# Converting each weight block one step earlier, and one subtraction moved from VectorE to GpSimd

## The chip, the cores and the metric

The kernel runs on one core of a Trainium2 chip. The metric is device time in microseconds (us) of one execution; the median of the runs shown is compared. Engines go by the profile's names: PE (TensorE), PEld (its weight loads), ACT (ScalarE), DVE (VectorE), POOL (GpSimd), SP (SyncE, which issues the DMAs).

## The reference, cut to what matters

Attention within clusters is followed by two dense layers. Softplus sits between the two matrices of the first layer, a hard swish between those of the second. All data come as float64.

```python
mask = q_assign[:, :, :, None] == k_assign[:, :, None, :]
attn = softmax(where(mask, q @ k.T / sqrt(D), -1e9));  x = attn @ v     # 2 x 8 heads, 768 tokens, D = 64
x = (1536, 512)
x = softplus(x @ w_in) @ w_out                                          # 512 -> 2048 -> 512
h = x @ w_in2;  out = (h * clip(h + 3, 0, 6) / 6) @ w_out2              # 512 -> 2048 -> 512
```

## The kernel before

The attention runs first (about 0 to 268 us of the span), the first layer then to about 531 us, the second to the end.

**The layers.** The 1536 tokens are cut into 3 blocks of 512 and the 2048 hidden columns into 16 blocks of 128, f = 0 to 15. A step is one (layer, token block, f); there are 96, numbered n. In step n PE does `phase_a(n)`, 12 matmuls from x to the hidden block h, and then `phase_b(n - 2)`, 12 matmuls from the hidden block of two steps before to the output accumulators y. Every product of two float32 numbers is made of three passes: high times high, low times high, high times low. So each hidden block and each weight block is needed as a high part and a low part. In `phase_b` the third matmul is the first that reads the low part `glo` of the hidden block.

**The hidden block.** In the first layer ACT applies softplus twice (`g` and `ghi`, L830 and L831) and DVE subtracts to get `glo` (L844). In the second layer ACT, DVE, ACT and DVE work in turn (L833, L837, L841, L844).

**The weights** come as float64 pairs of 32-bit words (tiles `ri`, `ro` for block f of the first and the second matrix) and are converted on the chip. One conversion is, for each of the two matrices: `convert_abs` (ACT, L98), three `convert_bits` (DVE, L106, L108, L112), `convert_parts` (ACT, L122, the high part), `convert_rest` (L133, the low part by a subtraction). The results are `pi` and `po`. Blocks 0 to 2 of the first layer are converted during the attention, where L133 runs on POOL. Blocks 3 to 15 are converted in the first layer's first token block, block f in step f - 2, and those of the second layer in steps 38 to 59, about one in every 1.4 steps. In these 29 conversions both L133 run on DVE.

**The order.** `convert_at` says which block is converted in which step. The loop over n (L905 to L948) emits the work of a step in this order: `phase_a(n)`; L133 and the rest of the second matrix left over from the last step (`late`); bits, high part and low part of this step's first matrix (`ci`); bits of its second matrix (`co`); softplus; `convert_abs` for the next step; the last bits of `co`; and after all that `hid_lo(t)`, the DVE subtraction for `glo` of step n. `with tc.manual_schedule()` keeps that order on each engine, within the attention and within the layers. Between the two regions a scheduler merges the queues by what is ready. So the first steps of the layers run among the last instructions of the attention. Step 0 and step 1 have their `phase_a` done inside the attention. The softplus of every step is held behind the last transposed copy of the attention on ACT (`issue_after(last_flip[0].ins)`).

The fetches of blocks 7 to 15 (L90, on SP) stand before the loop, and their tiles lie where attention tiles lay. The pool of the converted words (`val1`) has four buffers, two for each conversion.

Of the kernel before, what the change touches and what calls it, by code (L numbers as in the profile page):

```python
# [22 lines left out]
def cluster_attention_then_two_mlps(  # L23
# [13 lines left out]
    nc = tc.nc  # L37
# [43 lines left out]
    def fetch_w(layer, f):  # L81

        w_in, w_out = (w_in1, w_out1) if layer == 0 else (w_in2, w_out2)
        pool = wpa if f < NFA else wpools["b" if f < NFB else "c"]
        for nm, src in (
            ("i", w_in.bitcast(U32)[:, 2 * f * P:2 * (f + 1) * P].rearrange("(c p) f -> p c f", p=P)),
            ("o", w_out.bitcast(U32)[f * P:(f + 1) * P, :].rearrange("p (c e) -> p c e", c=NC)),
        ):
            w = pool.tile([P, NC, P, 2], U32, tag=f"w{nm}{f}", name=f"r{nm}{f}")
            nc.sync.dma_start(w.rearrange("p c e w -> p c (e w)"), src)  # L90
            pieces[layer, f, nm] = [w]

    def convert_abs(layer, f, nm):


        w = pieces[layer, f, nm]
        val = wpools["val"].tile([P, NC, P], F32, tag="val", name="val")
        nc.scalar.activation(val, w[0].bitcast(F32)[:, :, :, 1], AF.Copy, scale=2.0**-112)  # L98
        w.append(val)
# [50 lines left out]
    def phase_a(n, c):  # L150
        layer, tb, f = steps[n]
        if c == 0:
            pl, tag = (ps_p, "prep") if n % 4 == 0 else (ps_h[0], "h")
            hs[n] = pl.tile([P, 512], F32, tag=tag, name="h")
        hi_w, lo_w = weights[layer, f, "i"]
        cols = slice(tb * TB, (tb + 1) * TB)
        for i, (w, x) in enumerate(((hi_w, xhi), (lo_w, xhi), (hi_w, xlo))):
            nc.tensor.matmul(  # L158
                hs[n][:, :TB], w[:, c, :], x[c][:, cols], start=(c == 0 and i == 0), stop=(c == NC - 1 and i == 2)
            )  # L160
# [666 lines left out]
    def hid_scalar(t):  # L827

        if t["layer"] == 0:
            nc.scalar.activation(t["g"], t["h"], AF.Softplus)  # L830
            nc.scalar.activation(t["ghi"], t["h"], AF.Softplus)  # L831
        else:
            nc.scalar.activation(t["u"], t["h"], AF.Relu, bias=half, scale=1.0 / 6.0)  # L833

    def hid_gate(t):
        if t["layer"] == 1:
            nc.vector.scalar_tensor_tensor(t["g"], t["u"], 1.0, t["h"], ALU.min, ALU.mult)  # L837

    def hid_hi(t):
        if t["layer"] == 1:  # L840
            nc.scalar.activation(t["ghi"], t["g"], AF.Copy)  # L841

    def hid_lo(t):
        nc.vector.tensor_tensor(t["glo"], t["g"], f32(t["ghi"]), ALU.subtract)  # L844

    def hidden(layer, h):
        t = {"h": h, "layer": layer}
        t["ghi"] = tmp.tile([P, TB], F32R, tag="ghi", name="ghi")
        t["glo"] = tmp.tile([P, TB], F32R, tag="glo", name="glo")
        t["g"] = tmp.tile([P, TB], F32, tag="g", name="g")  # L850
        if layer == 1:
            t["u"] = tmp.tile([P, TB], F32, tag="u", name="u", bufs=2)
        return t

    def phase_b(layer, f, g, ys):
        ghi, glo = g["ghi"], g["glo"]
        hi_w, lo_w = weights[layer, f, "o"]
        terms = ((hi_w, ghi), (lo_w, ghi), (hi_w, glo))
        for e, y in enumerate(ys):
            for n, (w, x) in enumerate(terms):  # L860
                fl = dict(start=(f == 0 and n == 0), stop=(f == NF - 1 and n == 2))
                if layer == 0:
                    nc.tensor.matmul(y[:, :TB], w[:, e, :], x, **fl)  # L863
                else:
                    nc.tensor.matmul(y, x[:, e * P:(e + 1) * P], w.rearrange("p c e -> p (c e)"), **fl)  # L865

    def finish_block(layer, tb, ys):
        cols = slice(tb * TB, (tb + 1) * TB)
        if layer == 0:
            for e in range(NC):  # L870
                y = ys[e][:, :TB]
                nc.scalar.activation(xhi[e][:, cols], y, AF.Copy)
                nc.vector.tensor_tensor(xlo[e][:, cols], y, f32(xhi[e][:, cols]), ALU.subtract)
        else:
            for t in range(TB // P):
                o = wpools["val"].tile([P, DM], F32, tag="val", name="o")
                if t % 2:
                    nc.vector.tensor_copy(o, ys[t])
                else:
                    nc.scalar.activation(o, ys[t], AF.Copy)  # L880
                c = tb * (TB // P) + t
                nc.sync.dma_start(out_v[c // NJ, c % NJ], o)
# [2 lines left out]

    convert_at = {}
    for f in range(NFA + 0, NF):
        convert_at.setdefault(f - 2, []).append((0, f))
    for f in range(NF):
        convert_at.setdefault((NB - 1) * NF + LAG + 4 + (7 * f) // 5, []).append((1, f))  # L890
    for f in range(NFB, NF):
# [1 line left out]
    with tc.manual_schedule():  # L893
        gs, ysd = {}, {}
        late = None
        pend = lambda n: {nm: (l, f, nm) for l, f in convert_at.get(n, ()) for nm in "io"}
        nxt = pend(0)
        for c in nxt.values():
            convert_abs(*c)

        def do(fn, x, *a, **kw):
            if x is not None:
                fn(*x, *a, **kw)

        for n in range(len(steps) + LAG):  # L905
            cur, nxt = nxt, pend(n + 1)
            ci, co = cur.get("i"), cur.get("o")
            ni, no = nxt.get("i"), nxt.get("o")
            t = None
            if n < len(steps):  # L910
                if n not in hs:
                    for c in range(NC):
                        phase_a(n, c)
                t = gs[steps[n]] = hidden(steps[n][0], hs.pop(n)[:, :TB])

            do(convert_parts, late, False)
            do(convert_bits, ci, 0)
            do(convert_bits, ci, 1)
            do(convert_rest, late, engine=nc.vector)
            do(convert_bits, ci, 2)  # L920
            do(convert_parts, ci, False)
            do(convert_bits, co, 0)
            do(convert_bits, co, 1)
            if t:

                with tc.issue_after(last_flip[0].ins):
                    hid_scalar(t)
            do(convert_rest, ci, engine=nc.vector)
            do(convert_abs, ni)
            if t:  # L930
                hid_gate(t)
            do(convert_bits, co, 2)
            if t:
                hid_hi(t)
                hid_lo(t)
            do(convert_abs, no)
            late = co
            if n >= LAG:
                l, tb, f = s = steps[n - LAG]
                if f == 0:  # L940
                    ysd[l, tb] = [
                        ps_y.tile([P, 512], F32, tag=f"y{e}", name=f"y{e}") for e in range(NC)
                    ]
                phase_b(l, f, gs.pop(s), ysd[l, tb])
                if l == 0 and tb == NB - 1:
                    fetch_w(1, f)
                if f == NF - 1:
                    finish_block(l, tb, ysd.pop((l, tb)))  # L948
# [35 lines left out]
```

## Time and profile before

| | |
|---|---|
| median of 3 runs | 793.37 us (793.04 to 794.87) |
| profiled execution | 795.4 us, its span 793.6 us |
| PE, DVE, ACT, POOL busy | 97%, 58%, 52%, 20% of the span |
| DVE in 300 to 350 us | 39.52 of 50 us |
| POOL after 272 us | nothing |

Durations of the trace are those of the one profiled execution. Instructions of one engine overlap a little in the records (a DVE subtraction of 512 columns lasts 0.68 us, and the next one starts 0.60 us after it), so that the distance between starts says what an instruction costs its engine. PE's matmuls are pipelined: one of 512 columns is recorded with 0.39 us, and they start 0.23 us apart.

### The profile page before, as it was taken

The page shows a single profiled execution, that of the slowest core. Times are in us where ns is not written, and L with a number is a line of the kernel's source. Part 1 is how long each engine was busy: PE and PEld are TensorE (multiplying, and loading weights), DVE is VectorE, ACT ScalarE, POOL GpSimd, SP SyncE. Part 2 cuts the span into 40 slices and gives each one's busy share as a digit, 9 for nine tenths or more (in the row PEclk, how much of TensorE's full clock was granted, in tenths as well). Part 3 has the DMA queues.
Part 4 walks back from the last instruction along what each step waited for, and adds up shares of the span by engine and source line. Part 5 has one row for each costly group of instructions (what it writes and reads, how often), then busy time and mean ns, then how long its engine had stood idle before and what let it go on. Part 6 is the DMA issues. An engine that isn't in the chain of part 4 may idle for free.

```text
span 793.6 us, 10533 instructions
## 1 busy us (share of the span) xinstructions
PE 772.8 (97%) x3829; PEld 645.7 (81%) x3829; DVE 462.1 (58%) x793; ACT 413.8 (52%) x827; POOL 155.0 (20%) x225
## 2 busy tenths in 40 slices
PE   6799999999999999999999999999999999999998
PEld 5688888888888778888888888888888888888886
DVE  4888888888898899921111257779852322232222
ACT  3689889889899766532121344555432222222221
POOL 3467568568423300000000000000000000000000
PEclk8899999999999999999999999999999999999999
DMA  6675484484375390000000265650000100010001
GB/s 156 192 202 136 127 193 110 128 198 109 83 173 190 127 370 1 1 0 1 1 0 1 82 208 178 196 185 1 1 1 0 54 1 0 1 54 0 1 1 53
DMA packets 37876, 69.75 MB, mean 88 GB/s; under 512 B 4384, under 2 KB 22464, under 8 KB 37824
## 3 DMA queue, kind: packets, MB, share of 16 engines
q1 hardware_dynamic: 37488, 68.91, 30.2%
q8 instruction: 30, 0.49, 0.2%
q10 hardware_dynamic: 336, 0.16, 0.1%
q14 instruction: 22, 0.18, 0.1%
HBM read 46.30 MB, written 3.19 MB: 62 GB/s over the span
## 4 chain that ended last, share of the span: by engine, by line
PE 85%; ACT 5%; DVE 4%; DMA 3%; issue 1%; POOL 1%; SPq 0%; ACTq 0%; DVEq 0%; POOLq 0%
PE h L158 32%; PE y L865 17%; PE y L863 16%; PE s L397 6%; PE t L427 6%; PE pv L442 6%; PE psm L297 2%; ACT pr L413 2%; DMA Q<-hiq 1%; ACT pth L431 1%; DMA K<-hik 1%; ACT mk L356 1%; DVE val L108 1%; ACT xs L455 0%; ACT xs L457 0%
## 5 line engine op out<-in xcount | busy, mean ns | idle before, releaser
L158 PE MATMUL h<-xhi,pi 128*128 128x512 f32 x768 | 238.8, 392 | 2.2 <-DVE pi L133 2.2
L158 PEld LDWEIGHTS h<-xhi,pi 128*128 128x128 f32 x768 | 143.7, 188 | 34.3 <-DVE pi L133 3.0
L844 DVE TENSOR_TENSOR glo<-g,ghi 128x512 fp32r<-128x512 f32 x96 | 66.3, 691 | 146.3 <-ACT ghi L831 117.5
L158 PE MATMUL h<-xlo,pi 128*128 128x512 f32 x384 | 150.0, 391 | 0.0
L863 PE MATMUL y<-ghi,po 128*128 128x512 f32 x384 | 118.9, 391 | 0.0
L865 PE MATMUL y<-po,ghi 128*128 128x512 f32 x384 | 118.8, 391 | 0.0
L432 DVE TENSOR_TENSOR ptl<-t,pth 128x384 fp32r<-128x384 f32 x192 | 97.9, 549 | 31.8 <-ACT pth L431 31.6
L837 DVE SCALAR_TENSOR_TENSOR g<-u,h 128x512 f32<-128x512 f32 x48 | 33.0, 687 | 127.2 <-ACT u L833 127.2
L833 ACT ACTIVATE u<-h,half 128x512 f32<-128x512 f32 x48 | 33.0, 686 | 128.3 <-PE h L158 128.1
L397 PE MATMUL s<-K,Q 128*128 128x256 f32 (+1 forms) x384 | 91.8, 361 | 4.5 <-ACT pr L413 3.2
L431 ACT ACTIVATE pth<-t 128x384 fp32r<-128x384 f32 x192 | 85.3, 487 | 17.7 <-PE t L427 17.3
L405 DVE TENSOR_REDUCE nm<-s 128x1 f32<-128x768 f32 x96 | 90.6, 944 | 3.1 <-PE s L397 3.0
L427 PE MATMUL t<-ident,pr 128*128 128x128 f32 x576 | 88.4, 282 | 2.1 <-DVE ptl L432 1.4
L413 ACT ACTIVATE pr<-s,nm 128x768 f32<-128x768 f32 x96 | 86.5, 901 | 3.6 <-DVE nm L405 3.3
L830 ACT ACTIVATE g<-h 128x512 f32<-128x512 f32 x48 | 28.5, 594 | 111.1 <-PE h L158 111.1
L863 PEld LDWEIGHTS y<-ghi,po 128*128 128x128 f32 x384 | 72.0, 188 | 15.7
L158 PEld LDWEIGHTS h<-xlo,pi 128*128 128x128 f32 x384 | 72.1, 188 | 15.6
L865 PEld LDWEIGHTS y<-po,ghi 128*128 128x128 f32 x384 | 72.1, 188 | 15.5
L427 PEld LDWEIGHTS t<-ident,pr 128*128 128x128 f32 x576 | 65.3, 142 | 19.7 <-DVE ptl L432 15.1
L397 PEld LDWEIGHTS s<-K,Q 128*128 128x128 f32 x384 | 67.0, 192 | 15.9 <-ACT pr L413 5.4
L865 PE MATMUL y<-po,glo 128*128 128x512 f32 x192 | 75.1, 391 | 0.0
L863 PE MATMUL y<-glo,po 128*128 128x512 f32 x192 | 75.0, 391 | 0.0
(125 smaller groups left out, 945.8 us busy)
## 6 DMA issues: line engine op xcount, KB each, us to landing
ri<-in_moe_w_in SPq DMA_DIRECT2D x32, 512.0 KB, 4.7
ro<-in_moe_w_out SPq DMA_DIRECT2D x32, 512.0 KB, 5.3
K<-hik SPq DMA_DIRECT2D x31, 192.0 KB, 4.7
Q<-hiq SPq DMA_DIRECT2D x15, 384.0 KB, 4.2
Q<-loq SPq DMA_DIRECT2D x16, 192.0 KB, 5.6
v<-in_v SPq DMA_DIRECT2D x8, 384.0 KB, 3.4
rsb<-row SPq DMA_DIRECT2D x16, 192.0 KB, 4.0
out<-o SPq DMA_DIRECT2D x12, 256.0 KB, 2.0
```

The lines of the kernel that those rows point to most:

```text
L158: nc.tensor.matmul(hs[n][:, :TB], w[:, c, :], x[c][:, cols], start=(c == 0 and i == 0), stop=(c == NC - 1 and i == 2))
L397: nc.tensor.matmul(ps[:, n0:n1], Q[i][:, u, j * P:(j + 1) * P], K[i][:, u, n0:n1], start=(u == 0), stop=(u == 1),)
L405: nc.vector.tensor_reduce(nm, st_s[t][:, :S], AX.X, ALU.max, negate=True)
L413: nc.scalar.activation(pr, st_s.pop(t)[:, :S], AF.Exp, bias=st_p[t], accum_out=sums_of[n][:, i, j:j + 1])
L427: nc.tensor.transpose(pt[:, c * P:(c + 1) * P], pr[:, kt * P:(kt + 1) * P], ident)
L431: last_flip[:] = [nc.scalar.activation(dh, src, AF.Copy)]
L432: nc.vector.tensor_tensor(dl, src, f32(dh), ALU.subtract)
L442: nc.tensor.matmul(st_v[h][:, :HALF], vs[:, kt, i, :], st_t[h][u][:, kt, :], start=(kt == 0 and u == 0), stop=(kt == NJ - 1 and u == 1),)
L833: nc.scalar.activation(t["u"], t["h"], AF.Relu, bias=half, scale=1.0 / 6.0)
L844: nc.vector.tensor_tensor(t["glo"], t["g"], f32(t["ghi"]), ALU.subtract)
L863: nc.tensor.matmul(y[:, :TB], w[:, e, :], x, **fl)
L865: nc.tensor.matmul(y, x[:, e * P:(e + 1) * P], w.rearrange("p c e -> p (c e)"), **fl)
```

## The change

`convert_at` puts blocks 3 to 15 of the first layer one step earlier: block f is converted in step f - 3, block 3 in step 0 instead of step 1. Its two `convert_abs` then stand ahead of the loop. The second layer's places stay as they were. In addition, the low part of the second matrix (`po`, for `late`) is made on POOL instead of DVE, in both layers.

```diff
     for f in range(NFA + 0, NF):
-        convert_at.setdefault(f - 2, []).append((0, f))
+        convert_at.setdefault(f - 3, []).append((0, f))
...
             do(convert_bits, ci, 1)
-            do(convert_rest, late, engine=nc.vector)
+            do(convert_rest, late, engine=nc.gpsimd)
             do(convert_bits, ci, 2)
```

## Rows read from the trace of the kernel before

**Rows 1.** The page, parts 1 and 4: busy time by engine; chain by engine.

```profile
PE 772.8 (97%) x3829; PEld 645.7 (81%) x3829; DVE 462.1 (58%) x793; ACT 413.8 (52%) x827; POOL 155.0 (20%) x225
...
PE 85%; ACT 5%; DVE 4%; DMA 3%; issue 1%; POOL 1%; SPq 0%; ACTq 0%; DVEq 0%; POOLq 0%
```

**Rows 2.** Waits of PE, 270 to 420 us: total, times, longest.

```profile
PE h L158 <- DVE pi L133: 2.2, 2, 1.1
```

**Rows 3.** Timeline of PE, 268 to 280 us: start, us, line, tiles, idle before.

```profile
268.69 0.62 PE L863 MATMUL y<-ghi,po 128*128 128x512 f32 x2
269.16 0.40 PE L863 MATMUL y<-glo,po 128*128 128x512 f32 x1
...
271.45 0.39 PE L158 MATMUL h<-xhi,pi 128*128 128x512 f32 x1
272.90 0.50 PE L158 MATMUL h<-xhi,pi 128*128 128x512 f32 x1 [1.06 <-DVE pi L133]
...
279.79 0.50 PE L158 MATMUL h<-xhi,pi 128*128 128x512 f32 x1 [1.10 <-DVE pi L133]
```

**Rows 4.** Timeline of DVE, 285 to 291 us, one step.

```profile
285.39 0.68 DVE L844 TENSOR_TENSOR glo<-g,ghi 128x512 fp32r<-128x512 f32 x1
...
287.06 0.68 DVE L133 TENSOR_TENSOR po<-val,po 128x512 fp32r<-128x512 f32 x1
287.66 0.69 DVE L112 SCALAR_TENSOR_TENSOR val<-ri,val 128x512 uint32<-128x512 uint32 x1
...
290.53 0.68 DVE L844 TENSOR_TENSOR glo<-g,ghi 128x512 fp32r<-128x512 f32 x1
```

**Rows 5.** Chain in order of time, two halves of a PE step.

```profile
290.93 2.80 PE h L158 x12
...
329.33 2.72 PE h L158 x12
```

**Rows 6.** Stretches: length, busy PE, PEld, DVE, ACT, POOL, clock, DMA.

```profile
255.00:260.00 5.00, 4.72 (x28) 3.59 (x27) 4.06 (x9) 4.57 (x11) 0.72 (x1) 1.00 0.00 0
260.00:265.00 5.00, 4.94 (x27) 3.88 (x25) 3.81 (x9) 4.32 (x8) 2.64 (x4) 1.00 0.00 0
...
500.00:600.00 100.00, 100.00 (x440) 82.21 (x439) 73.66 (x124) 49.62 (x84) 0.00 (x0) 1.00 0.22 69
...
265.60:337.00 71.40, 69.24 (x305) 56.34 (x304) 70.51 (x122) 44.61 (x84) 4.38 (x3) 1.00 0.38 139
```

**Rows 7.** Timeline of POOL, the same instruction alone and beside DVE.

```profile
249.99 1.28 POOL L133 TENSOR_TENSOR po<-val,po 128x512 fp32r<-128x512 f32 x1 [5.64 <-ACT po L122]
...
267.45 1.79 POOL L133 TENSOR_TENSOR po<-val,po 128x512 fp32r<-128x512 f32 x1 [4.81 <-ACT po L122]
269.20 2.63 POOL L506 TENSOR_TENSOR xlo<-xs,xhi 128x384 fp32r<-128x384 f32 x2
```

**Rows 8.** Timeline of DVE, 267 to 273 us, beside the POOL rows above.

```profile
267.39 0.69 DVE L112 SCALAR_TENSOR_TENSOR val<-ri,val 128x512 uint32<-128x512 uint32 x1
268.00 1.52 DVE L106 TENSOR_SCALAR val<-val 128x512 uint32<-128x512 uint32 x1
269.56 1.39 DVE L108 SCALAR_TENSOR_TENSOR val<-ro,val 128x512 uint32<-128x512 uint32 x1
270.88 1.37 DVE L460 TENSOR_TENSOR xs<-xs,xs 128x384 f32<-128x384 f32 x1
272.17 0.68 DVE L133 TENSOR_TENSOR pi<-val,pi 128x512 fp32r<-128x512 f32 x1
...
285.99 0.42 DVE L106 TENSOR_SCALAR val<-val 128x512 uint32<-128x512 uint32 x1
286.44 0.69 DVE L108 SCALAR_TENSOR_TENSOR val<-ri,val 128x512 uint32<-128x512 uint32 x1
```

**Rows 9.** Timeline of DVE, after the last bits of block 15.

```profile
336.76 0.68 DVE L844 TENSOR_TENSOR glo<-g,ghi 128x512 fp32r<-128x512 f32 x1
```

**Rows 10.** Timeline of PE, third matmul of step 14's second half.

```profile
337.78 0.39 PE L863 MATMUL y<-glo,po 128*128 128x512 f32 x1
```

## Prediction

> **What bounds the kernel now.** I read the busy times first, then the chain, then the waits of PE, then the timelines around the place where they point. PE is busy for 97% of the span and has 85% of the chain [rows 1]; so the change can only give back time in which PE stands still. From 270 to 420 us PE waited for one thing alone: twice for the low part of a first matrix `pi` (L133 on DVE), 2.2 us together [rows 2]. The timeline shows the places. Matmuls start 0.23 us apart, so the one after 271.45 was due at 271.68 and came at 272.90, 1.22 us late; the same happened to the one at 279.79, and since its recorded idle is 0.04 us longer I take 1.26 [rows 3]. These are blocks 3 and 4. Together 2.48 us, and that is the most that an earlier conversion can return. The layers after it have no wait of PE that the change touches.
>
> Why are the two late? From 265.6 to 337 us DVE is busy 70.51 of 71.40 us [rows 6]: it works off the 13 conversions without a pause. Its step is 290.53 - 285.39 = 5.14 us between two `glo` [rows 4]. PE's step is two halves of 2.80 us while the weights come in and of 2.72 us later, that is 5.60 and 5.44 us [rows 5]. So DVE is only 0.3 to 0.5 us a step faster than PE, and whatever slows it by more than that makes it the bound of this stretch.
>
> **Part 1, POOL takes one subtraction.** DVE loses one L133 per step, which costs it 287.66 - 287.06 = 0.60 us [rows 4]. POOL needs 1.28 us for the same instruction [rows 7] and is otherwise idle; `po` is needed only four steps later, so POOL's slowness itself costs nothing. What counts is what the POOL instruction does to DVE. The only place of this trace where POOL subtracts while DVE is working through conversions is 267.45 to 271.83 us. The POOL subtraction took 1.79 us instead of 1.28 [rows 7]. On DVE, L112 had started just before it and kept its 0.69 us; the next one, L106, took 1.52 us where 0.42 is normal, and ended 0.28 us after the POOL instruction did. Then L108 took 1.39 us against 0.69, and L460 1.37 us, 1.29 to the next start, each beside one of the two POOL instructions L506 [rows 7, 8]. So the two engines take turns: the one that is in goes through, the other stands. In distance between starts L106 cost 269.56 - 268.00 = 1.56 us against 286.44 - 285.99 = 0.45, so one POOL subtraction of 512 columns cost DVE 1.11 us [rows 8]; I take 1.10. The bounds: 0 if DVE came through as L112 did (less than nothing has no row and no reason), and the whole 1.28 us. I stay with 1.10, since it is the same instruction at the same size. Then a step of DVE is 5.14 - 0.60 + 1.10 = 5.64 us, 0.50 more than before and no longer below PE's 5.60 and 5.44.
>
> On this the Trainium skill has a rule, in "SBUF — State Buffer", section "SBUF: two separate sides": VectorE and GpSimd share a pair of ports, which one of them holds for its whole instruction while the other is fully blocked, and this includes VectorE instructions with two SBUF inputs. The trace agrees with the taking of turns; for the size the rule would have the full 1.28 us of [rows 7] rather than 1.10, and the sum below, 3.4 us, would be 12 x 0.18 = 2.2 us larger, the time 799.0.
>
> **Part 2, one step earlier.** On ACT, the two `convert_abs` of block 3 and its `convert_parts` now stand ahead of the softplus of step 0. On DVE a step's order is conversion first, `glo` last. So `pi` of block f now has one `glo` less in front of it. But `glo` of step n, which PE reads in step n + 2, now stands behind the conversion of block n + 3 instead of n + 2. The wait of PE moves from `pi` to `glo`, and the lead of a step is gone again: PE's `phase_b(n)` can't pass its third matmul before DVE has done conversions 3 to n + 3 and `glo` 0 to n. No DMA moves in its queue. Blocks 7 to 15 are fetched from before the loop, and the bits of the first of them begin four DVE steps (4 x 5.14 = 20 us) after those of block 3; I cost that at nothing.
>
> **The sum.** I take the last `glo` that stands behind a conversion: that of step 12, behind block 15. Before, DVE had done exactly this work (blocks 3 to 15 and `glo` 0 to 12) when the `glo` of step 13 started, at 336.76 [rows 9]; with the 0.08 us by which an instruction outlasts the distance of starts (0.68 - 0.60) it ended at 336.84. After the change 12 subtractions (`po` of blocks 3 to 14) leave it, 12 x 0.60 = 7.2 us, and 12 turns of POOL come in, 12 x 1.10 = 13.2 us: 342.84. Against this stands what DVE can do before 265 us, since block 3 is now free to start among the last steps of the attention. DVE idles 5 - 4.06 = 0.94 us from 255 to 260 and 5 - 3.81 = 1.19 us from 260 to 265 [rows 6]; 2.1 us is the upper bound, 0 the lower (block 3 not pulled ahead). The three bits of block 3's first matrix cost 0.45 (285.99 to 286.44), 0.62 (286.44 to 287.06) and 0.60, 1.67 us [rows 4, 8], and fit there; I take 1.7. So `glo` of step 12 ends at 341.14, and 0.05 us later (as 272.17 + 0.68 to 272.90 [rows 3, 8]) PE can go on: 341.19. Before, PE ran that matmul at 337.78 [rows 10]. The change makes it later by 3.4 us. Behind it no conversion is left in the block and DVE soon catches up, so PE runs without a wait from there, and the 3.4 us stay to the end.
>
> In these 3.4 us the old 2.48 us are included: without any wait PE would be at 335.30, so the new waits for `glo` should add up to 5.9 us, spread from 269 to 336 us, the larger share early. I expect about 2 us at the first `phase_b` steps already, since PE wanted `glo` of step 0 at 269.16 [rows 3], and DVE has the attention's tail and three POOL instructions to get past then.
>
> In the second layer's conversions (16 more POOL subtractions) DVE loses the same 0.50 us each, 8 us in all, but it is busy there for 73.66 of 100 us [rows 6], and 8 us spread over some 120 us are covered by that idle time. If the cover were gone, it would be these 8 us.
>
> The sum is made in the profiled execution (795.4 us, span 793.6), which would become 798.8. The median of the runs, 793.37, is 2.0 us under it; I move it by the same 3.4 us: 796.8.
>
> **Rivals.** For all of them the shift is 3.4 + 12 x (price of a POOL turn - 1.10) - (work pulled ahead - 1.7), and at least -2.5. What a measurement of this kernel can tell from no change is about 0.3%, 2.4 us.
>
> *POOL shares rather than blocks, and the time falls.* If a POOL subtraction cost DVE 0.60 us or less, as much as it takes off, DVE would keep its 5.14 us step, both waits would vanish, and the time would be 793.4 - 2.5 = 790.9. It is faster at all below a price of 0.82. For it: L112 of [rows 8] lost nothing. Against it: the two behind it lost 1.1 and 0.7 us.
>
> *The turns are partly covered.* POOL may often get its turn where DVE waits anyway; at 0.90 us a turn the shift is +1.0, that is 794.4, no change. For it: the attention's tail is irregular. Against it: DVE has 0.9 us idle in 71 us [rows 6].
>
> *Block 3 isn't pulled ahead.* If the merge of the two regions leaves its conversion where it was (because the buffer of its words is free only when the attention's last tiles are), part 1 works and part 2 does nothing: 3.4 + 1.7 = 5.1, 798.5. For it: ACT is busy for 4.57 and 4.32 of 5 us there [rows 6], and softplus waits in the same queue.
>
> **How the numbers follow.** Slower by 2.4 us or more (a turn of 1.02 to 1.28 us, 796 to 799): 0.50. Block 3 not pulled ahead: 0.08. Partly covered, within 2.4 us: 0.32. Full gain: 0.10, of which some lies just within 0.3%. So slower 0.58, same 0.34, faster 0.08. The likeliest case has 795.8 to 799.0 for itself. The range, 791.9 to 799.5, takes in the covered cases and most of the bounds of the two unknown costs (1.28 us a turn gives 799.0).
>
> **What would show it.** Right: DVE instructions of 1.4 to 1.6 us beside each L133 on POOL from 268 to 337 us; a DVE step near 5.64 us; PE waiting at L863 for `glo` (L844) instead of at L158 for `pi`. Wrong: PE without a wait after 268 us, or DVE instructions that keep their 0.42 and 0.69 us beside POOL, or waits of PE for `pi` that stay.

## The result and the profile after

The changed kernel takes 798.74 us (median of 4 runs, 797.8 to 799.6) against 793.96 us for the kernel before on the same chip (median of 4 runs, 793.04 to 794.87). The ratio is 1.0058 with a 95% interval of 1.0044 to 1.0072, that is 4.6 us (3.5 to 5.7) more. It is slower, as forecast: 796.8 us had been forecast (3.4 us more), in a range of 791.9 to 799.5.

The page after, parts 1 and 4, which answer to [rows 1].

```profile
PE 776.3 (97%) x3829; PEld 645.9 (81%) x3829; DVE 465.7 (58%) x764; ACT 413.8 (52%) x827; POOL 197.9 (25%) x254
...
PE 86%; ACT 6%; DMA 3%; DVE 3%; issue 1%; POOL 1%; SPq 0%; ACTq 0%; DVEq 0%; POOLq 0%
```

DVE has 29 instructions less and yet 3.6 us more of busy time: what is left on it became longer. POOL has 42.9 us more.

The waits of PE and of its weight loads from 255 to 420 us in the changed kernel (columns as in [rows 2]).

```profile
PE y L863 <- ACT ghi L831: 1.8, 1, 1.8
PE y L863 <- DVE glo L844: 1.1, 1, 1.1
...
PEld y L863 <- DVE glo L844: 4.9, 13, 1.5
PEld y L863 <- ACT ghi L831: 2.3, 1, 2.3
```

The waits for `pi` of [rows 2] are gone. In their place the second half of a step (L863) waits. PE itself stood twice, once for softplus (`ghi`) and once for `glo`; its weight loads waited 13 times for `glo`, once for each of the first 13 steps' hidden blocks. One DVE step of the changed kernel, and POOL beside it:

```profile
283.89 0.69 DVE L844 TENSOR_TENSOR glo<-g,ghi 128x512 fp32r<-128x512 f32 x1
284.49 0.42 DVE L106 TENSOR_SCALAR val<-val 128x512 uint32<-128x512 uint32 x1
284.94 0.69 DVE L108 SCALAR_TENSOR_TENSOR val<-ri,val 128x512 uint32<-128x512 uint32 x1
285.67 1.66 DVE L112 SCALAR_TENSOR_TENSOR val<-ri,val 128x512 uint32<-128x512 uint32 x1
287.25 0.41 DVE L106 TENSOR_SCALAR val<-val 128x512 uint32<-128x512 uint32 x1
...
289.51 0.68 DVE L844 TENSOR_TENSOR glo<-g,ghi 128x512 fp32r<-128x512 f32 x1
```

```profile
285.13 1.65 POOL L133 TENSOR_TENSOR po<-val,po 128x512 fp32r<-128x512 f32 x1 [4.71 <-DMA ri<-in_moe_w_in]
```

L112 takes 1.66 us where it had 0.69 in [rows 4]; it ends 0.55 us after the POOL subtraction has ended. The step is 289.51 - 283.89 = 5.62 us. Taken over the eleven steps from the `glo` of step 1 to that of step 12 it is (340.22 - 278.25) / 11 = 5.63 us; forecast 5.64, before 5.14.

```profile
278.25 0.68 DVE L844 TENSOR_TENSOR glo<-g,ghi 128x512 fp32r<-128x512 f32 x1
...
340.22 0.69 DVE L844 TENSOR_TENSOR glo<-g,ghi 128x512 fp32r<-128x512 f32 x1
```

So a turn of POOL costs DVE 5.63 - 5.14 + 0.60 = 1.09 us. The forecast had read 1.10 off L106; here L108 is the instruction held in the first two turns and L112 in the other ten, at the same price.

The start of the layers on PE, which answers to [rows 3], and on ACT:

```profile
269.80 0.73 PE L863 MATMUL y<-ghi,po 128*128 128x512 f32 x2 [1.85 <-ACT ghi L831]
271.61 0.50 PE L863 MATMUL y<-glo,po 128*128 128x512 f32 x1 [1.08 <-DVE glo L844]
```

```profile
260.87 0.66 ACT L98 ACTIVATE val<-ri 128x512 f32<-128x512 f32 x1
...
265.71 0.63 ACT L122 ACTIVATE pi<-val 128x512 fp32r<-128x512 f32 x1 [0.66 <-ACT po L122]
...
267.37 1.28 ACT L830 ACT_TABLE_LOAD   x1
268.66 0.60 ACT L830 ACTIVATE g<-h 128x512 f32<-128x512 f32 x1
```

The softplus of step 0 stands behind `convert_parts` of block 3 (L122). That one starts when the last bits from DVE are done (265.62; the profile names an ACT instruction, which had ended before):

```profile
264.93 0.69 DVE L112 SCALAR_TENSOR_TENSOR val<-ri,val 128x512 uint32<-128x512 uint32 x1
```

Two instructions of the attention and the loading of softplus's table follow, and softplus starts at 268.66. In the kernel before, the same ACTIVATE was at 263.35:

```profile
263.35 0.60 ACT L830 ACTIVATE g<-h 128x512 f32<-128x512 f32 x1
```

And TensorE's granted clock, in stretches of 1 us of the changed kernel (columns as in [rows 6]):

```profile
271.00:272.00 1.00, 0.39 (x2) 0.35 (x3) 0.97 (x3) 0.63 (x1) 0.25 (x1) 1.00 1.03 395
273.00:274.00 1.00, 1.00 (x4) 0.71 (x4) 0.96 (x2) 0.00 (x0) 0.04 (x1) 0.50 1.06 371
276.00:277.00 1.00, 1.00 (x6) 0.78 (x6) 1.00 (x3) 1.00 (x3) 0.00 (x0) 1.00 1.08 399
```

PE had stood 2.93 of the 3.66 us from 267.95 to 271.61. From about 272 us the clock was at 0.50, the lower of its two levels (1.2 GHz), for some 3.4 us, and matmuls started 0.43 us apart instead of 0.23.

**A common zero.** Between two executions the first 260 us differ by up to 2.4 us, between kernels with the same attention too. So the traces below are laid on each other at the last transposes of the attention on PE (before and after):

```profile
260.95 0.49 PE L427 MATMUL t<-ident,pr 128*128 128x128 f32 x3
```

```profile
259.89 0.49 PE L427 MATMUL t<-ident,pr 128*128 128x128 f32 x3
```

The table gives, for each kernel, how much later than in the kernel before PE starts the second half (`phase_b`) of hidden block m, counted from that point; m = 18 lies behind the last conversion of the first layer. Of the runs it gives the ratio and its interval, and the shift in us that the ratio means. The columns by m come from one profiled execution of each kernel. Those of softplus first and of the memset were 1.4 and 1.2 us faster than the median of their runs, so that there the two kinds of column differ most.

| kernel | m = 0 | m = 4 | m = 12 | m = 18 | runs: ratio (95%), us |
|---|---|---|---|---|---|
| the change, both parts | +2.17 | +2.97 | +4.23 | +4.40 | 1.0058 (1.0044 to 1.0072), +4.6 |
| earlier only | +2.16 | +3.49 | +3.49 | +3.49 | 1.0041 (1.0029 to 1.0054), +3.3 |
| POOL only | +0.02 | +0.69 | +1.96 | +2.15 | 1.0032 (1.0020 to 1.0045), +2.5 |
| softplus first in step 0 | -0.01 | +5.90 | +5.90 | +5.90 | 1.0090 (1.0074 to 1.0107), +7.1 |
| POOL in the second layer only | +0.02 | +0.01 | +0.01 | +0.01 | 1.0011 (1.0003 to 1.0020), +0.9 |
| earlier only, PE kept at work | +2.24 | +2.48 | +2.48 | +2.48 | 1.0028 (1.0018 to 1.0039), +2.2 |
| both, PE kept at work | +2.23 | +3.03 | +4.25 | +4.44 | 1.0054 (1.0040 to 1.0068), +4.3 |
| both subtractions on POOL | +2.17 | +5.22 | +10.46 | +11.14 | 1.0148 (1.0135 to 1.0162), +11.8 |
| second matrix one step behind | -0.03 | -2.43 | -2.43 | -2.43 | 0.9974 (0.9964 to 0.9985), -2.1 |
| memset in the place of POOL's subtraction | +2.17 | +1.85 | +1.85 | +1.85 | 1.0035 (1.0023 to 1.0047), +2.8 |

### The profile page after: what moved, and what is told of

It is laid out like the page before. It is cut to its first block, busy times and chain, and to the rows that moved or that the text cites. A ratio compares the mean times of both kernels' runs of the same rounds, so it can differ in the third digit from the quotient of the medians.

```text
span 796.9 us, 10584 instructions
## 1 busy us (share of the span) xinstructions
PE 776.3 (97%) x3829; PEld 645.9 (81%) x3829; DVE 465.7 (58%) x764; ACT 413.8 (52%) x827; POOL 197.9 (25%) x254
## 4 chain that ended last, share of the span: by engine, by line
PE 86%; ACT 6%; DMA 3%; DVE 3%; issue 1%; POOL 1%; SPq 0%; ACTq 0%; DVEq 0%; POOLq 0%
PE h L158 32%; PE y L863 17%; PE y L865 17%; PE s L397 6%; PE pv L442 6%; PE t L427 6%; PE psm L297 2%; ACT pr L413 2%; DMA Q<-hiq 1%; ACT pth L431 1%; ACT xs L455 1%; DMA K<-hik 1%; ACT mk L356 1%; DMA K<-mk 0%; ACT val L98 0%
## 5 line engine op out<-in xcount | busy, mean ns | idle before, releaser
L844 DVE TENSOR_TENSOR glo<-g,ghi 128x512 fp32r<-128x512 f32 x96 | 66.5, 693 | 145.4 <-ACT ghi L831 116.6
L863 PE MATMUL y<-ghi,po 128*128 128x512 f32 x384 | 120.3, 395 | 1.8 <-ACT ghi L831 1.8
L133 POOL TENSOR_TENSOR po<-val,po 128x512 fp32r<-128x512 f32 x32 | 46.9, 1465 | 289.0 <-ACT po L122 143.2
L863 PEld LDWEIGHTS y<-ghi,po 128*128 128x128 f32 x384 | 72.6, 189 | 17.7 <-ACT ghi L831 2.3
L863 PE MATMUL y<-glo,po 128*128 128x512 f32 x192 | 76.9, 401 | 1.1 <-DVE glo L844 1.1
```

What stands on the lines that cost most here:

```text
L133: engine.tensor_tensor(lo, val, f32(hi), ALU.subtract)
```

## The experiments

**Earlier only.** The changed kernel with the subtraction back on DVE.

```diff
-            do(convert_rest, late, engine=nc.gpsimd)
+            do(convert_rest, late, engine=nc.vector)
```

> Only the earlier conversion (block f in step f - 3), all subtractions on DVE. Theory: the loss is the turns of POOL on a DVE that has no idle time, so without them DVE keeps its step of 5.14 us and stays ahead of PE; what remains is the wait at the first second half (1.85 + 1.08 us in the changed kernel) in place of the old two waits for pi (2.48 us): about +0.4 us on the kernel before, 794.3. Rival: the earlier place itself costs, by the softplus that waits behind block 3 in ACT's queue and the glo behind one more conversion: then +4 or more stays, about 798.

Measured +3.3 us, 797.02: the theory fell. The rival was right that the earlier place itself costs, though not quite its +4. The waits of PE (1.85 for `ghi`, 1.04 for `glo`) are those of the changed kernel, and the clock stood at 0.50 here too, for some 6.8 us:

```profile
273.00:274.00 1.00, 1.00 (x4) 0.71 (x4) 1.00 (x3) 0.96 (x2) 0.00 (x0) 0.50 1.08 432
```

DVE's step is 5.14 us and from m = 4 on nothing is added, so DVE without POOL's turns keeps up.

**POOL only.** The kernel before with the other half of the change.

```diff
-            do(convert_rest, late, engine=nc.vector)
+            do(convert_rest, late, engine=nc.gpsimd)
```

> Only the subtraction of the second matrix on POOL, block f still in step f - 2. Theory: DVE's step grows by 0.49 us (1.09 for a turn of POOL, less 0.60), over 12 steps 5.9 us; the pi of block 15 had 4.0 us in hand before, so PE comes 1.9 us later: 795.8, with waits of PE for pi (L133 on DVE) through the whole block and none for glo. Rival: the start-up makes the loss, not POOL: then 793.9, no change.

Measured +2.5 us, in the trace +2.15. As the theory has it, PE's weight loads waited 13 times for `pi`, in all 6.5 us against 3.0 us twice in the kernel before, and never for `glo`:

```profile
PEld h L158 <- DVE pi L133: 6.5, 13, 2.0
```

**Softplus first in step 0.** The changed kernel; the softplus and the `glo` of step 0 stand ahead of block 3's conversion, and its two `convert_abs` behind them.

```diff
...
+            if n == 0:
+                with tc.issue_after(last_flip[0].ins):
+                    hid_scalar(t)
+                hid_lo(t)
+                for c in cur.values():
+                    convert_abs(*c)
             do(convert_parts, late, False)
...
-            if t:
+            if t and n:
...
-                hid_lo(t)
+                if n:
+                    hid_lo(t)
```

> The changed kernel, but in step 0 softplus and the glo of the hidden block are queued ahead of block 3's conversion. Theory: DVE's work up to the glo of step 12 is the same, so the end stays where it is, at 798 to 800, though the wait at the first second half (2.9 us) is gone; PE waits for glo later and more often instead. Rival: the start-up wait of 2.9 us adds to the rest, and without it the time is 795.8.

800.83 us, a ratio of 1.0090 against the change's 1.0058: the rival is out, and the theory too. The end did not stay where DVE's work up to step 12 sets it. The whole +5.90 is there by m = 4 and POOL's turns add nothing to it, and the weight loads waited for `glo` once instead of 13 times. The wait at m = 0 is gone, but larger ones stand a step later, since the softplus of step 1 still is behind block 4's `convert_parts`. The clock stood at 0.50 here too, from about 277 us on for some 6.8 us.

```profile
271.01 0.50 PE L158 MATMUL h<-xhi,pi 128*128 128x512 f32 x1 [1.04 <-DVE pi L133]
276.21 0.73 PE L863 MATMUL y<-ghi,po 128*128 128x512 f32 x2 [2.37 <-ACT ghi L831]
279.12 0.80 PE L863 MATMUL y<-glo,po 128*128 128x512 f32 x1 [2.18 <-DVE glo L844]
```

**POOL in the second layer only.**

```diff
-            do(convert_rest, late, engine=nc.vector)
+            do(convert_rest, late, engine=nc.gpsimd if late and late[0] else nc.vector)
```

> The kernel before, with the subtraction on POOL in the second layer's 16 conversions only. Theory: DVE instructions grow to 1.6 us beside POOL there too, but DVE idles a quarter of that stretch, so no change, 793.9 within 0.5 us. Rival: a late glo reaches PE in the steps with conversions in a row, up to 8 us (16 x 0.49): 795 to 802.

The trace shows what the theory says: the first matrix's L112 grew to 1.22 us in the mean, and PE had no wait in the second layer. It agrees with the kernel before to 0.01 us at m = 18, and its span of 791.6 us, with 2.0 us less ahead of the common zero, ends at the same point as the 793.6 of before. The runs say +0.9 us with an interval of 0.2 to 1.6; where that came from the trace doesn't show, and it stays open.

```profile
L112 DVE SCALAR_TENSOR_TENSOR val<-ri,val 128x512 uint32<-128x512 uint32 x15 | 18.4, 1224 | 0.5
```

**Earlier only, PE kept at work.** Nine matmuls without use stand ahead of the first second half.

```diff
+                if n == LAG:
+                    for _ in range(9):
+                        nc.tensor.matmul(
+                            ysd[l, tb][3][:, :TB], weights[0, 0, "i"][0][:, 0, :], xhi[0][:, :TB], start=True, stop=True
+                        )
                 phase_b(l, f, gs.pop(s), ysd[l, tb])
```

> Only the earlier conversion, as in the run that made +3.4 us, with nine idle matmuls (9 x 0.23 = 2.05 us, into an accumulator bank that is started afresh afterwards) put ahead of the first second half, where PE waits 1.85 us for softplus. Theory: of the 3.4 us some 2.5 us are TensorE's clock, which after that wait stood at 0.50 for 6 us (matmuls 0.43 us apart instead of 0.23); with PE kept at work the clock stays at 1.00 and the time falls to about +0.9: 794.5. Rival: the clock is no matter, the wait itself and DVE make the 3.4: 797.

795.99 us, between the two. The clock stayed at 1.00, and 1.0 us came back in the trace (3.49 to 2.48), not 2.5, because a wait appeared that the slow clock had hidden: `glo` of step 1, behind the conversion of block 4.

```profile
270.97 0.50 PE L863 MATMUL y<-glo,po 128*128 128x512 f32 x1 [1.10 <-DVE glo L844]
277.98 0.50 PE L863 MATMUL y<-glo,po 128*128 128x512 f32 x1 [1.20 <-DVE glo L844]
```

**Both parts, PE kept at work.** The same nine matmuls in the changed kernel.

> The changed kernel (both parts) with the same nine matmuls. Theory: the start-up loss and the turns of POOL don't add, the larger sets the end; DVE's work up to the glo of step 12 is what it was, so though the clock stays at 1.00 the time stays near that of the change, 797.5 to 799, with more waits for glo in the steps after 276 us. Rival: the losses add, and without the clock's share it is 2 us faster: 796.5.

798.06 us, as the theory has it. The clock stayed at 1.00, and still m = 18 comes at +4.44 against +4.40. So 1.0 us less of start-up loss, as in the part alone, changes nothing at the end here: the losses don't add, and DVE's work sets the end.

```profile
273.00:274.00 1.00, 1.00 (x6) 0.81 (x5) 1.00 (x2) 0.25 (x1) 0.00 (x0) 1.00 1.10 425
```

**Both subtractions on POOL**, in the first layer.

```diff
-            do(convert_rest, ci, engine=nc.vector)
+            do(convert_rest, ci, engine=nc.vector if ci and ci[0] else nc.gpsimd)
```

> The changed kernel with the subtraction of the first matrix on POOL as well, in the first layer. Theory: a second turn of POOL per step, DVE's step is 4.54 - 0.60 + 2 x 1.09 = 6.1 us; over 12 to 13 steps 5.9 to 6.4 us more, all of it seen by PE: 804 to 806. Rival: POOL's turns are covered or shared: at most 800.

805.73 us, inside the theory's range. A DVE step is 297.91 - 291.77 = 6.14 us, and two of its instructions are long:

```profile
291.77 0.68 DVE L844 TENSOR_TENSOR glo<-g,ghi 128x512 fp32r<-128x512 f32 x1
292.38 0.41 DVE L106 TENSOR_SCALAR val<-val 128x512 uint32<-128x512 uint32 x1
292.82 1.67 DVE L108 SCALAR_TENSOR_TENSOR val<-ri,val 128x512 uint32<-128x512 uint32 x1
...
296.31 1.68 DVE L112 SCALAR_TENSOR_TENSOR val<-ro,val 128x512 uint32<-128x512 uint32 x1
297.91 0.68 DVE L844 TENSOR_TENSOR glo<-g,ghi 128x512 fp32r<-128x512 f32 x1
```

**Second matrix one step behind.** A version of the kernel before that takes work out of the way of the first `pi`, instead of moving a whole block.

```diff
     for f in range(NFA + 0, NF):
-        convert_at.setdefault(f - 2, []).append((0, f))
+        convert_at.setdefault(f - 2, []).append((0, f, "i"))
+        convert_at.setdefault(f - 1, []).append((0, f, "o"))
     for f in range(NF):
-        convert_at.setdefault((NB - 1) * NF + LAG + 4 + (7 * f) // 5, []).append((1, f))
+        for nm in "io":
+            convert_at.setdefault((NB - 1) * NF + LAG + 4 + (7 * f) // 5, []).append((1, f, nm))
...
-        pend = lambda n: {nm: (l, f, nm) for l, f in convert_at.get(n, ()) for nm in "io"}
+        pend = lambda n: {c[2]: c for c in convert_at.get(n, ())}
```

> A version that should beat both: all on DVE, the first matrix of block f in step f - 2 as before, its second matrix a step later, in f - 1 (it is needed in step f + 2). DVE has the same work but 3 to 4 instructions less ahead of the pi of blocks 3 and 4. Theory: both waits for pi (2.48 us) go and nothing comes in: 791.2. Rival: DVE has no idle time, so the wait only moves to a glo or a po: 793.7.

791.76 us, 0.9974 of the kernel before: the best version here. Of PE's waits for `pi` only two short ones of the weight loads are left, and the whole 2.4 us came back by m = 4.

```profile
PEld h L158 <- DVE pi L133: 0.6, 2, 0.4
```

**A memset on POOL.**

```diff
+        if nm == "o" and (layer == 1 or f >= NFA):
+            engine.memset(f32(lo), 0.0)
+            return
         engine.tensor_tensor(lo, val, f32(hi), ALU.subtract)
```

> The changed kernel with a memset of the same tile on POOL in the place of the subtraction (this leaves out the low part of the second matrices), so that POOL writes the 512 columns and reads nothing. Theory: only the start-up loss is left, which was 3.4 us with DVE alone, since DVE's step falls to 4.54 us and a little: 797. Of DVE's instructions those with two inputs (L108, L112, L133, 0.69 us) keep their time beside it. Rival: any instruction of POOL stops DVE for as long as it lasts: then single DVE instructions grow by the length of the memset, the time being 797 to 798.5.

797.34 us, which lies in the theory and in the rival alike; the single instructions decide. The memset lasts 0.53 us, and DVE's subtraction for `glo` beside it keeps its time, with 0.68 or 0.69 us in every case. L106 kept its 0.42 us but for two of 0.50; L108, L112 and L133 never stood beside a memset.

```profile
282.11 0.53 POOL L134 MEMSET po<- 128x512 f32 x1 [4.13 <-ACT val L98]
```

```profile
281.92 0.69 DVE L847 TENSOR_TENSOR glo<-g,ghi 128x512 fp32r<-128x512 f32 x1
```

So the rival is out, and with m = 4 to 18 at one value the start-up loss alone is left. PE had the same two waits, 1.83 and 1.08 us (and one of 0.60 at 278), and yet the clock stayed at 1.00, and m = 18 came at +1.85 instead of the +3.49 of the earlier part alone.

```profile
273.00:274.00 1.00, 1.00 (x7) 0.80 (x6) 1.00 (x3) 0.58 (x2) 0.00 (x0) 1.00 1.14 397
```

## Why the prediction was right, and what was off

- **DVE is the bound of the stretch, and POOL's turns make it slower than PE.** Right. The step came out at 5.63 us (forecast 5.64). The same price explains POOL only (+2.15), both subtractions on POOL (6.14 us a step) and the growth from m = 4 to m = 18 in the change. Here the rule of "SBUF — State Buffer", section "SBUF: two separate sides", that the Trainium skill has, holds with its exception: it counts a VectorE instruction with two inputs only against a GpSimd one that reads, and the memset, which reads nothing, cost the `glo` beside it none of its 0.69 us. A whole instruction of 1.28 us [rows 7] was not the price: from 5.14 to 5.63 us a step it is 0.60 + 0.49 = 1.09.
- **The lead is gone again because `glo` stands behind one more conversion.** Right: the weight loads of L863 waited for L844 13 times, and nothing waited for `pi`. Keeping PE at work in the run with the earlier part alone made the second such wait visible.
- **The sum.** The term of 1.7 us, what DVE does for block 3 before 265 us, was about twice too large; the price of a turn was right. The `glo` of step 12 ended at 340.91 and PE went on 0.05 us later:

```profile
340.96 0.50 PE L863 MATMUL y<-glo,po 128*128 128x512 f32 x1
```

On the clock of the kernel before that is 342.02, 4.2 us after the 337.78 of [rows 10], where the forecast had 341.19. Without the term the forecast's sum is 5.1, so some 0.9 us were pulled ahead and not 1.7. PE lost 0.16 us more in the matmuls behind it, which makes the 4.40 of the table. Block 3's first `convert_abs` ran only at 260.87 (261.93 on the clock of the kernel before). Of its three bits DVE had done L106, and begun L108, when it came to the point at which `glo` of step 0 had stood before (265.60, that is 264.54 here):

```profile
262.81 0.42 DVE L106 TENSOR_SCALAR val<-val 128x512 uint32<-128x512 uint32 x1
...
264.21 0.68 DVE L108 SCALAR_TENSOR_TENSOR val<-ri,val 128x512 uint32<-128x512 uint32 x1
```

- **The start-up.** The forecast had the wait at the first second half at 2 us and for `glo`. It was 1.85 us for softplus and 1.08 for `glo`. That softplus waits in ACT's queue stood among the rivals, and I gave it no price. In the change it cost nothing beyond the sum, for DVE's work is the later of the two. That hid an error in the forecast's floor: by its formula, a shift of "at least -2.5" where POOL costs no more than it takes off, the earlier place alone would have been a gain of 2.5 us. Run alone it is 3.3 us slower. That the total came out in spite of this is luck: with a cheaper turn of POOL the time would not have fallen as the forecast says, for without any turn it did not.
- **The new waits** were to add up to 5.9 us. With the shift of 4.40 and the old 2.48 they are 6.9: PE stood 2.9 us at the first second half; the rest, some 4 us, I put down to the slow clock and to weight loads that waited for `glo`.
- **The clock** was not foreseen. Its part is shown by one pair of kernels: +3.49 with it and +2.48 when PE was kept at work, each from one execution. The runs say +3.3 and +2.2, but their intervals overlap. In the change itself the slow clock cost nothing at the end (+4.40 with it, +4.44 without).
- **The second layer** at nothing: right in the traces (in the change m = 18 and the end of the span are late by the same 4.4 us); in the runs of that part alone there are 0.9 us that no row explains.

## What to carry to other kernels

Moving an elementwise instruction from a saturated VectorE to an idle GpSimd took off its 0.60 us and put back 1.1 us here. Where VectorE had idle time, in the second layer, it cost nothing in the trace, but it brought nothing either; no run here shows a gain. An instruction of GpSimd that only writes left the subtraction beside it alone. Moving work one step ahead in a queue that is in order is paid by what now stands behind it: look which consumer comes after the moved work, and give each queue it goes through (here ACT's too) a price of its own. Where a producer is saturated, move less urgent work behind the urgent, as the second matrix here; it gave 2.1 us, most of what the change was after.

## What the runs showed of the hardware that was not expected

A wait of TensorE of about 2 us with another of 1 to 2 us close behind it went with a granted clock of 0.50 for 3.4 to 6.8 us in four of the traces (the change, the earlier part alone, softplus first, both subtractions on POOL). In the change the clock fell after the second wait; in the other three it fell before the second wait was over, some 0.6 to 0.8 us after the matmul that followed the first (1.85, 2.37 and 1.85 us). In the earlier part alone:

```profile
268.98 0.77 PE L863 MATMUL y<-ghi,po 128*128 128x512 f32 x2 [1.85 <-ACT ghi L831]
270.80 0.80 PE L863 MATMUL y<-glo,po 128*128 128x512 f32 x1 [1.04 <-DVE glo L844]
```

```profile
270.00:271.00 1.00, 0.20 (x1) 0.20 (x2) 1.00 (x3) 0.69 (x2) 0.00 (x0) 0.50 1.10 420
```

In a fifth trace with waits of 1.83 and 1.08 us (the memset) it stayed at 1.00. Two waits of 1.1 us, 7 us apart, as in the kernel before, did not bring it down. What decides it no run here tells.
